# Fused attention and two-layer product on one Trainium2 core: the tenth pair of heads turned by DMA instead of on the matmul engine, with four edits around it

## The chip, the cores and the metric

The kernel runs on one core of a Trainium2 chip. A core has five engines with instruction queues of their own, which meet only at semaphores: PE (TensorE, matrix products), DVE (VectorE), ACT (ScalarE), POOL (GpSimd) and SP (SyncE, which here only issues DMA transfers). Sixteen DMA engines move the data; SP and ACT feed one group of queues, POOL another. The metric is the device time of one execution in microseconds, lower is better.

## The reference

The input is q, k and v, each of 8 batches x 12 heads x 448 rows x 64, a number tau of 0.1, w_in (768 x 2048) and w_out (2048 x 768), all float32.

```python
q_n = q / (norm(q, axis=-1) + 1e-6)
k_n = k / (norm(k, axis=-1) + 1e-6)
scores = q_n @ k_n.T / tau
attn = softmax(scores)                 # over the keys of one head
x = (attn @ v), heads side by side     # 3584 rows x 768
h = x @ w_in
out = maximum(0.01 * h, h) @ w_out     # 3584 x 768, float32
```

## The kernel before

**Pairs and quads.** Heads are worked two at a time. A pair s holds q and k of two heads; a batch has six pairs (NPAIR), so the pairs of batch 0 are 0 to 5, those of batch 1 are 6 to 11, and so on: the "tenth pair" is s = 9, the "ninth" s = 8. Two pairs form a quad j of four heads (pairs 8 and 9 are quad 4). The 448 rows are three tiles of 128 and a remainder of 64 rows.

**What a pair goes through.** `load_qk` (four transfers on SP's queue) or `load_pairs` brings the rows to `raw_sb`, which has six places, one for each pair of a batch. `squares` squares them, on POOL by default. `sums` adds them up on DVE, `roots` takes the roots on ACT, and `normalise` on DVE multiplies the rows with the reciprocals into `qn`, in bf16. `transposes` turns `qn` so that the 64 columns lie on the partitions: for s below DMA_FROM by seven PE transposes into one PSUM bank and a copy from there into `qkT`, from DMA_FROM on by one DMA transpose that SP issues. `norm` is roots, normalise, transposes and squares of a later pair in a row; its `hold` makes POOL wait for the rows of `qn`, so that what POOL does next starts behind them.

**Scores and exponents.** `key_tiles` makes the scores of one key tile of a pair on PE (two banks of PSUM) and their exponents on ACT. Tile 3 is the remainder tile: it takes the 64 remaining keys of both pairs of a quad at once, and its exponents go to `pr[j]`. `attend` and `attend_two` multiply the exponents with v and with ones; `attend_two` does two quads and begins with the remainder products of both, alternating between them (L306, `rem_products`).

**The first product** (`firsts`, L383): for each of 16 column blocks m of w_in six matmuls, and ACT's leaky ReLU (`Prelu`) into `hT`. The dictionary `between` says which steps of later pairs are written ahead of which m. The order in which the program is written is the order on every engine's queue.

**The second product** (`visit` with `groups`, L458) works through hT x w_out for one batch of tokens. While it runs, the key tiles of the next batch are put between its matmuls: `wide`, for the first visit, says after which step n a tile is put; pair 6's tiles come first, then pair 7's and so on to pair 11's. The visit begins with remainder tiles of some quads and ends with the others, behind the output copies of its last group, the first of which runs on ACT. The first group of the first visit goes through w_out in four parts of four row blocks, steps 1 to 16, 17 to 32, 33 to 48 and 49 to 64.

**w_out** comes in four quarters (`load_w_out`), issued on POOL's queue: quarters 0 and 4 behind the quad 2 results, quarters 8 and 12 in `norm` of pairs 7 and 8. The numbers are those of each quarter's first row block. On each kind of queue a transfer also waits for the landing of the eighth before it, since there are eight semaphores to tell of landings.

**The stretch of the change** is from 35 us, where batch 0's attention has ended, to 72 us, where batch 1's begins: firsts(0) with the norms of pairs 6 to 10, then visit(0).

The diff touches:

Of the kernel before, what the change touches and what calls it, by code (L numbers as in the profile page):

```python
# [16 lines left out]
def kernel(  # L17
# [10 lines left out]
    nc = tc.nc  # L28
# [11 lines left out]
    KT = D_model // 128  # L40
    MT = D_ff // 128
    HALF = D_model // 2
    DMA_FROM = 10
    WARM = 20
    SOON = 4
    AHEAD = 3
# [28 lines left out]
    def banks(count, keep=None, which=None):  # L75
        lo, hi = (0, 8) if not deals["apart"] else (0, 4) if count == 2 else (4, 8)
        x = which if which is not None else min(
            (i for i in range(lo, hi, count) if not set(range(i, i + count)) & set(sum(kept.values(), []))),
            key=lambda i: max(age[i : i + count]),
        )  # L80
        deals["n"] += 1
        age[x : x + count] = [deals["n"]] * count
        if keep:
            kept[keep] = list(range(x, x + count))
        return ps[:, x] if count == 1 else ps[:, x : x + count]
# [23 lines left out]
    def load_w_out(parts):  # L109
        for m in parts:  # L110
            gp.dma_start(out=w_out_sb[:, m : m + MT // 4], in_=w_out_r[:, m : m + MT // 4])

    def main(x, b, h0, nh):
        return x[b, h0 : h0 + nh, 0:MAIN].rearrange("h (p t) d -> p h t d", t=3)
# [22 lines left out]
    def load_qk(s):  # L137
        if s >= NSLOT:
            return
        b, h0 = s // NPAIR, 2 * (s % NPAIR)  # L140
        both = raw_sb[:, s % NPAIR]
        nc.sync.dma_start(out=both[:, :, 0:3], in_=main(q, b, h0, 2))
        nc.sync.dma_start(out=both[:, :, 4:7], in_=main(k, b, h0, 2))
        for i, x in enumerate((q, k)):
            nc.sync.dma_start(
                out=both[64 * i : 64 * i + 64, :, 3],
                in_=x[b, h0 : h0 + 2, MAIN:S].rearrange("h p d -> p h d"),
            )
        raw[s] = (both[:, :, 0:4], both[:, :, 4:7])
# [5 lines left out]
    def load_v(j):  # L155
        if j >= B * NQ:
            return
        b, jj = divmod(j, NQ)
        vb[j] = vbp.tile([128, 4, 3, D], BF16, name="v_b")
        gp.dma_start(out=vb[j], in_=main(v, b, 4 * jj, 4))  # L160

    def load_v_rem(b, parts=slice(0, 4)):
        if b >= B:
            return
        x = vrb[b % 2].rearrange("p j g d -> p (j g) d")
        for lo, h0, h1 in ((0, 0, 2), (64, 2, 6), (0, 6, 10), (64, 10, 12))[parts]:
            gp.dma_start(  # L167
                out=x[lo : lo + 64, h0:h1], in_=v[b, h0:h1, MAIN:S].rearrange("h p d -> p h d")
            )
# [3 lines left out]
    def squares(s, engs=(gp, gp)):  # L173
        if s >= NSLOT:
            return
        tiles = []
        for x, eng, name in zip(raw[s], engs, ("sq0", "sq1")):
            sq = sqp.tile(list(x.shape), F32, name=name)
            if eng is nc.scalar:
                nc.scalar.activation(sq, x, func=AF.Square)  # L180
            else:
                eng.tensor_tensor(sq, x, x, op=ALU.mult)  # L182
            tiles.append(sq)
        sqs[s] = tiles

    def sums(s, parts=(0, 1)):
        if s >= NSLOT:
            return
        if s not in ss:
            ss[s] = smp.tile([128, 14], F32, name="ss")  # L190
        for i in parts:
            o = ss[s][:, 0:8] if i == 0 else ss[s][:, 8:14]
            nc.vector.tensor_reduce(  # L193
                o.rearrange("p (h t) -> p h t", h=2), sqs[s][i], axis=AX.X, op=ALU.add
            )

    def roots(s):
        if s >= NSLOT:
            return
        nc.scalar.activation(ss[s], ss[s], func=AF.Ln, bias=tiny)  # L200
        nc.scalar.activation(ss[s], ss[s], func=AF.Exp, scale=0.5)  # L201

    qn, scalings = {}, {}
# [30 lines left out]
    def one(tp, s, lo, hi):  # L234
        for t in range(lo, hi):
            nc.tensor.matmul(
                out=tp[:, t, :],
                lhsT=qn[s][:, t].rearrange("p h d -> p (h d)"),
                rhs=id128,
                is_transpose=True,  # L240
                start=(t == lo),
                stop=(t == hi - 1),
            )

    def transposed():
        return banks(1).bitcast(BF16)[:, : 7 * 128].rearrange("p (t c) -> p t c", c=128)

    def transposes(s):
        if s >= NSLOT:
            return  # L250
        dst = qtp.tile([128, 7, 128], BF16, name="qkT")
        qkT[s] = dst.rearrange("p t c -> p (t c)")
        if s >= DMA_FROM:
            nc.sync.dma_start(
                out=dst, in_=qn[s].rearrange("p t h d -> p (t h d)"), transpose=True
            )
            return
        tp = transposed()
        one(tp, s, 0, 7)
        nc.vector.tensor_copy(out=dst, in_=tp)  # L260

    pe, pr = {}, {}

# [3 lines left out]
    def key_tiles(which):  # L267

        tiles = []
        for s, ki in which:  # L270
            sc = banks(2)
            tiles.append(sc)
            for i in range(2 if ki == 3 else 1):
                x = qkT[s - 1 + (i ^ s // 2 % NQ % 2)] if ki == 3 else qkT[s]
                for a in range(2):
                    rows = slice(64 * a, 64 * a + 64)
                    out = sc[64 * i : 64 * i + 64] if ki == 3 else sc
                    c0, c1 = (448, 512) if ki == 3 else (512 + 128 * ki, 640 + 128 * ki)
                    nc.tensor.matmul(  # L279
                        out=out[:, a, :S], lhsT=x[rows, c0:c1], rhs=x[rows, 0:S],  # L280
                        start=True, stop=True,
                    )
        for (s, ki), sc in zip(which, tiles):
            if ki == 3:
                pr[s // 2] = prp.tile([128, 2, S], BF16, name="pr")
                dst = pr[s // 2]
            else:
                if s not in pe:
                    pe[s] = pep.tile([128, 3, 2, S], BF16, name="pe")
                dst = pe[s][:, ki]  # L290
            nc.scalar.activation(out=dst, in_=sc[:, :, :S], func=AF.Exp, scale=inv_tau)  # L291
# [219 lines left out]
    def hold(x):  # L511
        seen = smp.tile([128, 1], F32, name="seen")
        gp.tensor_copy(out=seen, in_=x)  # L513
# [28 lines left out]
    dst = qtp.tile([128, 7, 128], BF16, name="qkT")  # L542
    qkT[0] = dst.rearrange("p t c -> p (t c)")
    for lo, hi in ((0, 4), (4, 7)):
        tp = transposed()
# [153 lines left out]
    def norm(s, transposed=True):  # L699
        if s >= NSLOT:  # L700
            return
        roots(s)
        normalise(s)
        if transposed:
            transposes(s)
        if s == 10:
            return
        for x in (12, 13) if s == 11 else (s + 4,) if s > 11 else ():
            load_qk(x)
        hold(qn[s][:, 6, 0, 0:1])  # L710
        if s < 9:
            load_w_out((4 * (s - 5),))
        if s == 11:
            squares(12)
        if s != 9:
            squares(s + (3 if s < 9 else 2))
# [11 lines left out]
    def visit(b, order, norms, between):  # L728


        s0 = (b + 1) * NPAIR
        tiles = [(s0 + p, ki) for p in range(NPAIR) for ki in range(3)]
        key_tiles([(s0 + 1, 3), (s0 + 3, 3)] + [(s0 + 5, 3)] * (b > 1))
        for i, (pairs, after) in enumerate(zip(order, between)):
            last = i == len(order) - 1
            for n, _ in enumerate(groups(b, pairs, 4 if len(pairs) > 1 else 1, last), 1):
                for _ in range(after.get(n, 0)):
                    key_tiles([tiles.pop(0)])
                for fn in norms.get((i, n), ()):
                    fn()  # L740
        assert not tiles
        if b < 2:
            key_tiles([(s0 + 5, 3)])

    def at(*steps):
        return {n: steps.count(n) for n in steps}
# [7 lines left out]
    attend(NQ - 1, [lambda m=m: first(0, m, range(KT - 2)) for m in range(3, SOON)])  # L754
    normalise(6)
    hold(xT[0][:, 2 * NQ - 2, 0:1])
    load_w_out((0, 4))
    hold(qn[6][:, 6, 0, 0:1])
    squares(9)
    norm(7, False)  # L760
    sums(8)
    firsts(
        0, SOON, {
            4: [lambda: transposes(6), lambda: norm(8, False)],
            6: [lambda: sums(9)],
            7: [lambda: transposes(7)],
            9: [lambda: norm(9, False)],
            10: [lambda: transposes(8)],
            11: [lambda: sums(10), lambda: load_v(3)],
            12: [lambda: norm(10), lambda: load_v(4)],  # L770
            13: [lambda: transposes(9), lambda: load_v(5), lambda: load_v_rem(1)],
            15: [lambda: sums(11)],
        },
    )
# [1 line left out]
    for b in range(B):  # L776
# [26 lines left out]
        s = ready  # L803
# [57 lines left out]
```

## Time and profile before

| | us |
|---|---|
| runs | 410.4, 408.26, 410.38; median 410.38 |
| profiled execution | 408.75 |
| its span | 407.0 |
| PE busy | 397.6 (98% of the span) |
| ACT busy | 262.3 (64%) |
| DVE busy | 191.1 (47%) |
| POOL busy | 143.5 (35%) |
| granted TensorE clock | 1.0 throughout |

A line of the timeline or of the lists has the start in us, the time it covers, the engine, the line of the kernel, the operation, what is written and read, the shape and the count; behind it in brackets stands the idle time of the engine before it and what ended that. In the waits, the numbers are total us, count and longest. PE's busy time is modelled for pipelined matmuls, so that 98% says that PE has hardly an idle moment, not that it works at its peak. A line of the chain of waits has start, length and what the chain went through.

### The profile page before, as it was taken

What the parts mean: (1) busy time and instruction counts of PE and PEld (TensorE: products, weight loads), DVE (VectorE), ACT (ScalarE), POOL (GpSimd) and SP (SyncE); (2) the same over time, 40 slices, a digit from 0 to 9 for tenths busy, and PEclk for the clock granted to TensorE, in tenths of its full rate; (3) what the DMA queues carried; (4) which work ended last, traced back from release to release, by engine and by line L of the source; (5) the groups of instructions that cost most, each with busy time, mean ns of one, the idle gap of its engine ahead of it and who ended that gap; (6) DMA issues with size and microseconds to landing.
All of it is one profiled execution on the core that took longest, in us unless ns stands there. A gap on an engine that the chain in (4) does not pass through costs nothing.

```text
span 407.0 us, 10163 instructions
## 1 busy us (share of the span) xinstructions
PE 397.6 (98%) x4086; PEld 225.0 (55%) x4096; DVE 191.1 (47%) x405; ACT 262.3 (64%) x454; POOL 143.5 (35%) x218
## 2 busy tenths in 40 slices
PE   7899999999999999999999999999999999999996
PEld 2335655444555655544786555544687555544554
DVE  5987931775674715355463626256262631130021
ACT  4995589566865579645876569845776559844300
POOL 4997632374325414253141622255122500000000
PEclk9999999999999999999999999999999999999999
DMA  7999999599598936588396854685397821110033
GB/s 181 248 224 240 216 180 229 154 177 203 124 199 160 156 72 159 118 131 176 58 183 154 125 128 109 168 117 134 81 168 129 102 46 40 40 41 2 0 78 79
DMA packets 100735, 54.21 MB, mean 133 GB/s; under 512 B 69424, under 2 KB 95440, under 8 KB 100688
## 3 DMA queue, kind: packets, MB, share of 16 engines
q1 hardware_dynamic: 76400, 40.13, 43.3%
q0 software_dynamic: 23440, 12.92, 23.3%
q8 instruction: 32, 0.52, 0.5%
q10 hardware_dynamic: 848, 0.52, 0.4%
q14 instruction: 15, 0.12, 0.1%
HBM read 45.61 MB, written 11.01 MB: 139 GB/s over the span
## 4 chain that ended last, share of the span: by engine, by line
PE 88%; DVE 5%; POOL 3%; DMA 1%; issue 1%; ACT 1%; POOLq 0%
PE ps L383 33%; PE ps L458 31%; PE ps L319 11%; PE ps L279 8%; PE ps L420 5%; DVE qn L222 2%; POOL sq L182 1%; PE ps L306 1%; DMA raw_sb<-in_k_dram 1%; DVE ss L193 1%; POOL v_rem L167 1%; DVE r L218 0%; DVE qkT L260 0%; POOL raw_sb L132 0%; DVE ss L217 0%
## 5 line engine op out<-in xcount | busy, mean ns | idle before, releaser
L383 PE MATMUL ps<-xT,w_in_sb 128*128 128x384 bf16 (+1 forms) x760 | 147.6, 352 | 0.4
L458 PE MATMUL ps<-w_out_sb,hT 64*128 64x384 bf16 x1536 | 144.0, 323 | 0.0
L291 ACT ACTIVATE pe<-ps 128x896 bf16<-128x896 f32 x144 | 124.5, 917 | 17.9 <-PE ps L279 16.0
L383 PEld LDWEIGHTS <-w_in_sb 128*128 128x128 bf16 x768 | 74.1, 98 | 71.7 <-issue 4.0
L390 ACT ACTIVATE hT<-ps 128x384 bf16<-128x384 f32 (+1 forms) x128 | 66.8, 543 | 66.4 <-PE ps L383 65.9
L458 PEld LDWEIGHTS <-hT 64*128 64x128 bf16 x1536 | 84.4, 94 | 44.6 <-PE ps L458 4.2
L182 POOL TENSOR_TENSOR sq<-raw_sb 128x512 f32<-128x512 f32 x92 | 84.9, 944 | 14.8 <-DMA raw_sb<-in_k_dram 13.9
L222 DVE TENSOR_TENSOR qn<-raw_sb,r 128x512 bf16<-128x512 f32 x96 | 59.2, 658 | 1.6
L279 PE MATMUL ps<-qkT 64*128 64x448 bf16 (+1 forms) x384 | 55.0, 353 | 2.1 <-DVE qkT L260 1.6
L193 DVE TENSOR_REDUCE ss<-sq 128x6 f32<-128x384 f32 (+1 forms) x95 | 54.3, 610 | 1.1 <-POOL sq L182 1.1
L470 DVE COPY osb<-ps 128x384 f32<-128x384 f32 x41 | 21.2, 553 | 69.8 <-PE ps L458 38.9
L513 POOL CAST seen<-qn 128x1 f32<-128x1 bf16 x47 | 9.2, 197 | 123.0 <-DVE qn L222 122.5
L217 DVE TENSOR_SCALAR ss<-ss 128x14 f32<-128x14 f32 x48 | 9.8, 205 | 74.0 <-ACT ss L201 73.8
L360 DVE TENSOR_TENSOR xT<-ps,rb 128x448 bf16<-128x448 f32 x48 | 27.8, 620 | 24.6 <-ACT rb L339 24.4
L160 POOL DMA_DIRECT2D v_b<-in_v_dram x24 | 18.6, 778 | 39.9 <-PE ps L319 39.9
L319 PE MATMUL ps<-pe,v_b 128*32 128x448 bf16 x576 | 32.0, 353 | 0.0
L279 PEld LDWEIGHTS <-qkT 64*128 64x128 bf16 (+1 forms) x384 | 17.8, 97 | 18.7 <-issue 7.3
L338 ACT ACTIVATE rb<-ps 128x448 f32<-128x448 f32 x24 | 12.9, 538 | 14.9 <-PE ps L319 13.9
L426 DVE COPY osb<-ps 128x384 f32<-128x384 f32 (+1 forms) x9 | 4.6, 513 | 36.6 <-issue 22.6
L319 PEld LDWEIGHTS <-v_b 128*32 128x32 bf16 x576 | 15.2, 97 | 11.9 <-issue 0.6
L291 ACT ACTIVATE pr<-ps 128x896 bf16<-128x896 f32 x24 | 20.8, 923 | 0.4 <-PE ps L279 0.4
L420 PE MATMUL ps<-w_out_sb,hT 128*128 128x384 bf16 (+1 forms) x144 | 21.0, 308 | 0.0
(50 smaller groups left out, 185.9 us busy)
## 6 DMA issues: line engine op xcount, KB each, us to landing
raw_sb<-in_q_dram SPq DMA_DIRECT2D x46, 192.0 KB, 3.3
raw_sb<-in_k_dram SPq DMA_DIRECT2D x44, 192.0 KB, 3.1
out_dram<-osb SPq DMA_DIRECT2D x30, 192.0 KB, 3.0
v_b<-in_v_dram POOLq DMA_DIRECT2D x24, 192.0 KB, 4.7
out_dram<-osb SPq DMA_DIRECT2D x12, 384.0 KB, 2.7
w_out_sb<-in_moe_w_out_dram POOLq DMA_DIRECT2D x4, 768.0 KB, 13.7
w_in_sb<-in_moe_w_in_dram POOLq DMA_DIRECT2D x3, 512.0 KB, 9.0
w_in_sb<-in_moe_w_in_dram POOLq DMA_DIRECT2D x2, 768.0 KB, 13.7
```

The lines of the kernel that those rows point to most:

```text
L182: eng.tensor_tensor(sq, x, x, op=ALU.mult)
L193: nc.vector.tensor_reduce(o.rearrange("p (h t) -> p h t", h=2), sqs[s][i], axis=AX.X, op=ALU.add)
L222: scalings[s] = nc.vector.tensor_tensor(qn[s][:, lo:hi], x.rearrange("p h t d -> p t h d"), r[:, r0 : r0 + 2 * nt].rearrange("p (h t) -> p ...
L279: nc.tensor.matmul(out=out[:, a, :S], lhsT=x[rows, c0:c1], rhs=x[rows, 0:S], start=True, stop=True,)
L291: nc.scalar.activation(out=dst, in_=sc[:, :, :S], func=AF.Exp, scale=inv_tau)
L319: nc.tensor.matmul(out=x[32 * g : 32 * g + 32, :S], lhsT=weights(g, ki) if ki < 3 else rem(g), rhs=pe[s][:, ki, a, :] if ki < 3 else pr[j] ...
L360: scalings[j, e] = nc.vector.tensor_tensor(xT[m][:, 2 * jj + e, half * S : (half + 1) * S], pos.pop((j, e))[:, :S], rbs[j], op=ALU.mult,)
L383: nc.tensor.matmul(out=pm[:, :n], lhsT=w_in_sb[:, kt, m * 128 : (m + 1) * 128], rhs=xT[c // 2][:, kt, c0 : c0 + n], start=(kt == 0), stop= ...
L390: nc.scalar.activation(out=hT[c][:, m, :n], in_=pms.pop((c, m))[:, :n], func=AF.Prelu, alpha=0.01)
L420: nc.tensor.matmul(out=po2[:, :n], lhsT=hT[c][:, m, ts * 128 : (ts + 1) * 128], rhs=w_out_sb[:, m, lo : lo + n], start=(m == 0), stop=(m = ...
L458: done[p][i] = nc.tensor.matmul(out=pos2[p][:, i, :HALF], lhsT=hT[c][rows, m, ts * 128 : (ts + 1) * 128], rhs=w_out_sb[rows, m, half * HAL ...
L470: copy(out=osb[c, ts][:, half * HALF : (half + 1) * HALF], in_=po2[:, i, :HALF])
```

## The change

DMA_FROM goes from 10 to 9, so pair 9 is turned by a DMA that SP issues, right behind its normalise, and its seven PE transposes and its copy on DVE are gone. The copy of pair 8 is done by ACT. Pair 9's squares are done by ACT, ahead of firsts(0), instead of by POOL. The remainder tile of pairs 8 and 9 goes from the beginning of the first visit to its end, ahead of that of pairs 10 and 11. The four quarters of w_out are issued one behind the other, without the hold on pair 6's rows that stood behind the first two. The transposes of pairs 6 and 7 are written one block of m later.

```diff
-    DMA_FROM = 10
+    DMA_FROM = 9
...
         tp = transposed()
         one(tp, s, 0, 7)
-        nc.vector.tensor_copy(out=dst, in_=tp)
+        copy = nc.scalar.copy if s > 7 else nc.vector.tensor_copy
+        copy(out=dst, in_=tp)
...
         hold(qn[s][:, 6, 0, 0:1])
-        if s < 9:
-            load_w_out((4 * (s - 5),))
...
-        key_tiles([(s0 + 1, 3), (s0 + 3, 3)] + [(s0 + 5, 3)] * (b > 1))
+        rests = [(s0 + i, 3) for i in (1, 3, 5)]
+        early = 1 if b == 0 else 2 if b == 1 else 3
+        key_tiles(rests[:early])
...
-        if b < 2:
-            key_tiles([(s0 + 5, 3)])
+        if rests[early:]:
+            key_tiles(rests[early:])
...
     hold(xT[0][:, 2 * NQ - 2, 0:1])
-    load_w_out((0, 4))
-    hold(qn[6][:, 6, 0, 0:1])
-    squares(9)
+    load_w_out(range(0, MT, MT // 4))
     norm(7, False)
+    squares(9, (nc.scalar, nc.scalar))
     sums(8)
     firsts(
         0, SOON, {
-            4: [lambda: transposes(6), lambda: norm(8, False)],
+            4: [lambda: norm(8, False)],
+            5: [lambda: transposes(6)],
             6: [lambda: sums(9)],
-            7: [lambda: transposes(7)],
-            9: [lambda: norm(9, False)],
+            8: [lambda: transposes(7)],
+            9: [lambda: norm(9)],
             10: [lambda: transposes(8)],
             11: [lambda: sums(10), lambda: load_v(3)],
             12: [lambda: norm(10), lambda: load_v(4)],
-            13: [lambda: transposes(9), lambda: load_v(5), lambda: load_v_rem(1)],
+            13: [lambda: load_v(5), lambda: load_v_rem(1)],
             15: [lambda: sums(11)],
         },
     )
```

## The prediction

> **What bounds the kernel now.** I read the page first, then the waits of the matmul engine, then its timeline and the chain of waits around the first visit, then the DMA view by stages.
>
> The page gives the matmul engine 397.6 us of 407.0, so all that an edit can win there is idle time or matmuls taken away:
>
> ```profile
> span 407.0 us, 10163 instructions
> ...
> PE 397.6 (98%) x4086; PEld 225.0 (55%) x4096; DVE 191.1 (47%) x405; ACT 262.3 (64%) x454; POOL 143.5 (35%) x218
> ```
>
> The waits of PE over the whole span have one item that the change touches, 0.8 us for a VectorE copy of a turned pair; the 1.2 us for qn are transposes that came early:
>
> ```profile
> PE ps L279 <- DVE qkT L260: 1.6, 3, 0.8
> ...
> PE ps L236 <- DVE qn L222: 1.2, 2, 1.1
> ```
>
> PE's timeline just ahead of the first visit shows the place: pair 9's seven transposes, the last 18 matmuls of the first product, the remainder tile of pairs 6 and 7, a hole, the remainder tile of pairs 8 and 9, and the visit's first matmuls on w_out.
>
> ```profile
> 47.30 0.79 PE L236 MATMUL ps<-id,qn 128*128 128x128 bf16 x7
> 47.94 3.09 PE L383 MATMUL ps<-xT,w_in_sb 128*128 128x384 bf16 x18
> 50.95 0.38 PE L279 MATMUL ps<-qkT 64*64 64x448 bf16 x4
> 52.14 0.38 PE L279 MATMUL ps<-qkT 64*64 64x448 bf16 x4 [0.81 <-DVE qkT L260]
> ```
>
> The chain says who makes the hole: VectorE, which works through norm, sums and copies of pairs 6 to 11 in order and puts pair 9's copy behind pair 10's norm.
>
> ```profile
> 50.39 1.16 DVE qn L222 x2
> 51.55 0.54 DVE qkT L260
> 52.10 0.04 issue
> 52.14 0.38 PE ps L279 x4
> ```
>
> From 52.46 to 71.9 PE has no hole, but its inputs come late. The w_out quarters, issued at 35.73, 36.53, 41.12 and 47.22 on POOL's queue, took 12.4, 15.4, 14.5 and 12.9 us to land; the view of their tile gives the ends. The view of qkT in the same stretch has the two turns by DMA, of pairs 10 and 11. The DMA view of 56 to 59 us shows that the two queues then send equal numbers of packets:
>
> ```profile
> DMA to landing us min/median/max: 12.4/13.7/15.4
> ```
>
> ```profile
> DMA to landing us min/median/max: 7.1/8.7/10.3
> ```
>
> ```profile
> q0 software_dynamic: 508, 0.34, 87.5%
> q1 hardware_dynamic: 516, 0.13, 51.7%
> ```
>
> So the quarters land at 48.15, 51.9, 55.65 and 60.1: 3.75 us apiece, and 4.5 us for the last, the one that runs beside pair 10's turn (issued 51.62, landed 61.9). PE's first matmul on each stands, counted off its timeline, at 52.46, 55.45, 58.62 and 61.78: spare 4.3, 3.5, 3.0 and 1.7 us.
>
> **The change part by part.** *Before the visit.* Pair 6's transposes go one block later: they start at 37.15 and the next block at 37.75, 18 matmuls take 2.93 us (40.68 less 37.75), so the twelve from 35.02 end at 36.97, and 0.78 us become the 0.39 that the unwaited transposes of pairs 7 and 8 show (43.99 to 44.38): 0.39 saved. Pair 9's transposes go: 0.63 (47.31 to 47.94). The hole and the second remainder tile leave this place: rest tile at 50.95, group from 51.14 (two tiles in a row follow at 0.19, as 68.12 and 68.31 do) instead of 52.46, but with the drain that one tile shows, 0.31, at 51.3: about 1.2. Sum 2.2: the visit starts at 50.25, if its feeders keep up.
>
> They do. ScalarE's squares of pair 9, 0.63 + 0.52 us from the start-up's rows, fall in its hole from 35.21 to 36.37 (1.16); if the cover fails, Prelus queue behind them, with eight banks to spare. VectorE loses two copies (0.61 each) and the norm of pair 7 that took 2.63 us beside POOL's squares at 37.85 to 40.12 becomes the usual 1.16. That brings pair 9's norm from 47.7 to about 46.7, pair 10's from 51.5 to about 50.0, pair 11's sums to 51.1. Pair 8's copy on ScalarE, 0.59 + 0.48 in the start-up's halves, stands behind the roots of pair 9 and ends near 45.9; PE first reads pair 8's rows at step n = 40 of the visit. PE waits for neither. The remainder of pairs 6 and 7 needs the copy of pair 7, at 44.6.
>
> *w_out's quarters in a row.* On POOL two issues of 0.8 us leave the path of the squares of pairs 10 and 11, but those wait for their rows until 44.86 anyway (a wait of 2.92 in the trace). Each issue waits for the landing of the one eight before it, here the two w_in halves (issued 25.65 and 26.45, landed 37.8 and 41.6), so POOL is free at 42.4. The queue has work without a break from 24 us, 3.75 us a quarter: an earlier issue lands nothing earlier. Zero; from below, if some of the 0.75 us by which the last quarter is stretched were late issue, it would win that.
>
> *Pair 9's turn.* Issued on SP near 46.7, on an empty queue; the next on SP is pair 10's turn, ready 3.4 us later. Unloaded a turn takes 2.9 us from issue to landing (78.59 to 81.55), loaded it took 10.3 and 7.1. First packets come 3.9 us after the issue when loaded (pair 10's: 55.55), so near 50.6. A turn is 128 x 896 bf16 in packets of some 256 bytes (0.13 MB in 516), so 896, 56 for each of 16 engines; a quarter of w_out has 128 x 4 rows, 32 an engine, one each 0.117 us (3.75 / 32). Alternating one for one, the quarter beside pair 10's turn took 0.75 us longer, 0.023 a packet of the turn. So quarter three, now also beside a turn, lands at 52.1 + 4.5 = 56.6 and quarter four at 61.1; pair 9's turn ends near 58.6, needed near 61. Bounds for the added delay at quarter four: 0, if the turns fit into gaps, and 1.65 us, a whole unloaded transfer (2.9 less the 1.25 of its issue); I take 0.95 (61.1 less 60.14), by the row nearest to it.
>
> The Trainium skill, "VectorE: DVE Perf Modes", section "The three transpose paths", speaks against the change: it gives 390 ns on TensorE and 1309 ns by DMA for a 128 x 128 tile, so that seven tiles would take an estimated 9.2 us a turn. The trace's unloaded 2.9 us for all seven contradicts it as a sum of tiles; with it for each of three turns in a row the last would end past 74 us and the sum be over +7.
>
> PE would reach quarter three at 56.4 and four at 59.6. It waits 0.2, then 1.4 us: at that place it is 0.6 us ahead of before, not 2.2.
>
> *The remainder tile at the end.* Before, only pair 11's stood there, read much later. Now that of pairs 8 and 9 stands there too, and the next matmuls on PE, the remainder products of L306, read its exponents at once (the second one does: they alternate between the two quads). ScalarE's rows there:
>
> ```profile
> 70.92 0.94 ACT L291 ACTIVATE pe<-ps 128x896 bf16<-128x896 f32 x1
> 71.72 0.51 ACT L470 COPY osb<-ps 128x384 f32<-128x384 f32 x1
> 72.08 0.97 ACT L291 ACTIVATE pr<-ps 128x896 bf16<-128x896 f32 x1
> ```
>
> The tile's scores start on PE at 71.57 and an exponent in that slot ends at 73.05, 1.48 us later; before, L306 started 0.31 later. With some 0.05 to be seen, PE loses 1.2 us there, and the added tile's own 0.19 hides in it. Bounds: 0.8, if the output copy were quicker out of the way, to 1.6, if the score tile's bank is late. Behind that wait PE's queue holds all products of the second batch; the other exponent, pair 11's, follows on ScalarE while PE works on the remainder products. From there to the end nothing changes, and PE has no hole there that could swallow the delay.
>
> *Pair 11's turn* is issued with the visit, 2.2 us earlier (57.05), behind those of pairs 9 and 10 on SP: pair 10's lands near 63.6 (needed 65.8), pair 11's near 67.2, where PE wants it at 67.5. Before: 66.35 against 68.12. I take no wait. The loads of pairs 12 and 13, next on SP, come no later than before, and the squares of pair 12 (68.39) with them.
>
> Sum: −2.2 + 0.2 + 1.4 + 1.2 = **+0.6 us**.
>
> The profiled execution took 408.75 us (span 407.0, 1.75 around it); the three runs, 410.4, 408.26 and 410.38, have a median 1.6 above it. So 409.35 against the profiled one, 411.0 against the median. As the runs lie on two levels, and the profile is of the lower, I say 410.8.
>
> **The rivals.**
>
> *The gain comes through.* The turn costs w_out nothing and the earlier issues keep quarter four at 59.6 or before; then −2.2 + 1.2 = −1.0: 407.75 by the profile, 409.4 by the median. For it: pair 10's turn is the only one seen beside w_out, so the 0.75 us may belong to the late issue of that quarter and not to the turn. Against: the fourth quarter's 4.5 us beside a turn. Even if ScalarE's exponent cost nothing, it ends at −2.2. Chance 0.2.
>
> *The turns queue one behind another, slower than before.* If three turns in a row each take the 6.3 us from first packet to landing of pair 10's (55.55 to 61.89), pair 9's ends at 57.0, pair 10's at 63.3 and pair 11's at 69.6, where PE wants it at 67.5: 2.1 us more, +2.7 in all, 411.45 by the profile, 413.1 by the median. It decides as soon as pair 11's turn lands after 67.5, 10.5 us after its issue; the 7.1 of before is against it, the 10.3 of pair 10's for it.
>
> *The hole was no hole.* The change may do nothing because VectorE still sets the pace (its norm of pair 10 at 51.5): then the start stays near 52.4, no wait for w_out arises, and +1.2 remains: 409.95 or 411.6. Against: nothing of pair 9 or 10 is read before 61 any more. Chance 0.05.
>
> **How the numbers follow.** The forecast has 0.47, the rivals 0.2, 0.28 and 0.05. What a measurement of this kernel can tell from no change is about 0.5%, 2 us. The forecast lies inside it, 0.85 of it with the spread of the runs (0.1 above, 0.05 below); the first rival has 0.6 inside and 0.4 faster, only because a low level may meet the high median; the second 0.7 slower; the third 0.8 inside. Sum: faster 0.10, same 0.65, slower 0.25. The range takes in the first rival by the median less half the spread of the runs and the second by the median: 408.4 to 413.1.
>
> **What would show it.** Right: no L260 copy and no 0.81 hole near 50 us; the visit's first w_out matmul near 50.3; a PE wait for w_out's last quarter of about 1 us near 60; a wait of L306 on ScalarE's exponent of about 1 us near 71; everything after shifted by a constant. Wrong if the last quarter lands before 60, if pair 11's tiles wait, or if L306 does not.

## The result: 0.3% faster, and the profile after

Over 22 runs of each, the changed kernel has a median of 408.73 us (407.71 to 409.84) and the kernel before one of 410.31 us (408.26 to 411.28). The ratio is 0.9968, with a 95% interval of 0.9956 to 0.9979: 1.3 us less. (It is the ratio of the means; the medians lie 1.6 us apart, since four of before's 22 runs were near 408.4.) That is inside the 0.5% named as no change and inside the range, but the forecast was +0.6 us, a time of 410.8, and the sign is the other one.

The runs of before did not spread evenly. Over this result and the experiments below there were 89 of them: 17 lie between 407.97 and 408.76, 72 between 409.85 and 411.55, and none between. The profiled execution of before (408.75) is of the lower, rarer kind. The two levels turn out to decide the sign.

The page of the changed kernel, its first lines. The span stands where that of before's profiled execution stood (407.0), with PE 0.6 us busier:

```profile
span 407.1 us, 10160 instructions
...
PE 398.2 (98%) x4089; PEld 225.8 (55%) x4089; DVE 187.9 (46%) x403; ACT 263.8 (65%) x457; POOL 140.5 (35%) x215
```

The waits of its PE (total, count, longest). The 0.8 us for the turned pair's copy is gone; a wait for w_out and one for ScalarE's exponent have come:

```profile
PE ps L459 <- DMA w_out_sb<-in_moe_w_out_dram: 1.2, 1, 1.2
PE ps L307 <- ACT pr L292: 0.7, 1, 0.7
```

Its PE timeline at three places: the visit's start, w_out's last quarter, and the moved remainder tile (lines after the edit count one higher: L279 is L280, L306 is L307). The first matmul of the remainder products runs at 71.15, the second only at 72.17:

```profile
49.77 0.38 PE L280 MATMUL ps<-qkT 64*64 64x448 bf16 x4
50.08 1.47 PE L459 MATMUL ps<-w_out_sb,hT 64*128 64x384 bf16 x16
...
58.96 0.67 PE L459 MATMUL ps<-w_out_sb,hT 64*128 64x384 bf16 x6
60.85 0.50 PE L459 MATMUL ps<-w_out_sb,hT 64*128 64x384 bf16 x4 [1.22 <-DMA w_out_sb<-in_moe_w_out_dram]
...
70.64 0.57 PE L280 MATMUL ps<-qkT 64*64 64x448 bf16 x8
71.15 0.36 PE L307 MATMUL ps<-pr,ones 64*32 64x448 bf16 x1
72.17 0.38 PE L307 MATMUL ps<-pr,ones 64*32 64x448 bf16 x7 [0.67 <-ACT pr L292]
```

The chain of waits now goes through the last quarter of w_out (issued 41.87, 18.93 us under way) instead of VectorE, and at the visit's end through the output copy and the exponent, as the prediction's slot said:

```profile
41.87 18.93 DMA w_out_sb<-in_moe_w_out_dram
60.80 0.04 issue
...
70.93 0.37 ACT osb L471
71.30 0.83 ACT pr L292
```

The tiles' landings, first w_out's quarters (47.89, 51.70, 56.24, 60.80; before 12.4 to 15.4 us), then the three turns (pair 9's at 59.86, pair 10's at 64.51, pair 11's at 67.27; before 7.1 to 10.3):

```profile
DMA to landing us min/median/max: 12.6/16.9/18.9
```

```profile
DMA to landing us min/median/max: 10.3/12.5/13.9
```

And the two DMA queues from 52 to 55 us, where before only w_out was under way; now pair 9's turn sends packet for packet with it:

```profile
q0 software_dynamic: 348, 0.51, 93.8%
q1 hardware_dynamic: 348, 0.09, 22.1%
```

Measured from the first matmul of `firsts(0)` (34.60 here, 35.02 in before's profile), the visit's first w_out matmul comes 1.96 us earlier, w_out takes 1.22 back, 0.23 goes in the visit, and the remainder tile takes 1.22: L307 resumes 0.71 us later than L306 did. (The whole times, 408.88 and 408.75, differ by 0.13 only, as `firsts(0)` began 0.42 earlier.) Against the execution it was worked out on, the forecast of +0.6 came true. What it was worked out on was not the usual execution.

### The profile page after: what moved, and what is told of

The parts are those of the page before. It is cut to its first block, busy times and chain, and to the rows that moved or that the text cites. A ratio compares the mean times of both kernels' runs of the same rounds, so it can differ in the third digit from the quotient of the medians.

```text
span 407.1 us, 10160 instructions
## 1 busy us (share of the span) xinstructions
PE 398.2 (98%) x4089; PEld 225.8 (55%) x4089; DVE 187.9 (46%) x403; ACT 263.8 (65%) x457; POOL 140.5 (35%) x215
## 4 chain that ended last, share of the span: by engine, by line
PE 82%; DMA 10%; POOL 3%; ACT 2%; issue 1%; DVE 0%; SPq 0%; POOLq 0%
PE ps L384 32%; PE ps L459 28%; PE ps L320 10%; PE ps L280 6%; PE ps L421 5%; DMA w_out_sb<-in_moe_w_out_dram 5%; DMA w_in_sb<-in_moe_w_in_dram 3%; POOL sq L182 2%; ACT pe L292 1%; DMA raw_sb<-in_q_dram 1%; PE ps L307 1%; DMA raw_sb<-in_k_dram 1%; POOL raw_sb L132 0%; POOL v_rem L167 0%; DVE qn L222 0%
## 5 line engine op out<-in xcount | busy, mean ns | idle before, releaser
L459 PEld LDWEIGHTS <-hT 64*128 64x128 bf16 x1536 | 85.4, 94 | 44.9 <-PE ps L459 4.0
L182 POOL TENSOR_TENSOR sq<-raw_sb 128x512 f32<-128x512 f32 x90 | 82.5, 937 | 15.2 <-DMA raw_sb<-in_k_dram 14.4
L222 DVE TENSOR_TENSOR qn<-raw_sb,r 128x512 bf16<-128x512 f32 x96 | 57.5, 640 | 2.0 <-DMA raw_sb<-in_q_dram 0.3
L280 PE MATMUL ps<-qkT 64*128 64x448 bf16 (+1 forms) x384 | 55.0, 353 | 1.1 <-DVE qkT L261 0.6
L217 DVE TENSOR_SCALAR ss<-ss 128x14 f32<-128x14 f32 x48 | 9.5, 198 | 74.8 <-ACT ss L201 74.7
L280 PEld LDWEIGHTS <-qkT 64*128 64x128 bf16 (+1 forms) x384 | 17.9, 97 | 17.5 <-issue 7.0
```

Of the source, the lines that this page charges most:

```text
L222: scalings[s] = nc.vector.tensor_tensor(qn[s][:, lo:hi], x.rearrange("p h t d -> p t h d"), r[:, r0 : r0 + 2 * nt].rearrange("p (h t) -> p ...
L280: nc.tensor.matmul(out=out[:, a, :S], lhsT=x[rows, c0:c1], rhs=x[rows, 0:S], start=True, stop=True,)
L459: done[p][i] = nc.tensor.matmul(out=pos2[p][:, i, :HALF], lhsT=hT[c][rows, m, ts * 128 : (ts + 1) * 128], rhs=w_out_sb[rows, m, half * HAL ...
```

## The experiments

They ran in four groups, each with runs of the kernel before on the same chip, whose medians were 410.42, 410.50, 410.23 and 410.31 us. Two runs far off, of 1069 us (the profiled one of the squares on ScalarE) and of 1130 us (one of the first attempt to force the meeting), are left out; why they took so long was not found.

**Before, unchanged, profiled twice more.** The second kernel differs in a comment alone.

> The kernel before, unchanged, profiled once more, because its first profile (408.75 us) was of the lower of its two levels and most runs took about 410.3. Late-rows theory: where the time is near 410.3, the hole on PE ahead of the first visit is not 0.8 us but 2.5 to 3 us, because the rows of pairs 10 and 11 land later, their squares, sums and norm come later, and pair 9's copy stands behind that norm on VectorE. Rival theory (elsewhere): the 2 us lie at the start-up, in the granted clock or in a later stage, and the hole stays at 0.8 us.

> The same again (only a comment added), for a second look at the usual level. Late-rows theory: hole of 2.5 to 3 us if the time is near 410.3, 0.8 if it is near 408.5. Elsewhere theory: the hole is 0.8 us at either level.

The first took 410.31 us, the upper level, the second 408.45, the lower. The upper one has the same 0.80 us hole before the visit, and its rows do not come late: pair 10's landed earlier (43.57 against 44.63 in the lower profile). What it has more is at pair 9's transposes, which ran almost without a wait at the lower level. Its PE timeline:

```profile
48.22 0.40 PE L236 MATMUL ps<-id,qn 128*128 128x128 bf16 x4 [0.95 <-DVE qn L222]
49.32 0.34 PE L236 MATMUL ps<-id,qn 128*128 128x128 bf16 x3 [0.70 <-DVE qn L222]
```

They wait for `normalise` of pair 9, two multiplies on VectorE. Here are VectorE's and then POOL's lines at the upper level; POOL's squares there are those of pair 11:

```profile
45.97 3.30 DVE L222 TENSOR_TENSOR qn<-raw_sb,r 128x512 bf16<-128x512 f32 x2
```

```profile
45.70 0.81 POOL L111 DMA_DIRECT2D w_out_sb<-in_moe_w_out_dram  x1
46.53 2.31 POOL L182 TENSOR_TENSOR sq<-raw_sb 128x512 f32<-128x512 f32 x2
```

And the same at the lower level, from before's profile. There the rows of pair 10 came later, so POOL's squares of pair 11 came behind the norm and fell beside VectorE's sums instead:

```profile
46.24 1.46 DVE L222 TENSOR_TENSOR qn<-raw_sb,r 128x512 bf16<-128x512 f32 x2
...
48.16 1.13 DVE L193 TENSOR_REDUCE ss<-sq 128x8 f32<-128x512 f32 x2
```

```profile
48.05 1.83 POOL L182 TENSOR_TENSOR sq<-raw_sb 128x512 f32<-128x512 f32 x2
```

The norm takes 3.30 us beside POOL's squares of pair 11, 1.46 ahead of them, and for the longer one PE pays 1.65 us (0.95 + 0.70). So the late-rows theory falls, and a new one, the collision theory, stands: at the upper level pair 9's norm runs into POOL's squares; the changed kernel no longer turns pair 9 on PE, so nobody waits for that norm, and the upper level is gone. The rival: some other edit of the change brings the gain.

**The change in parts.** First the remainder tile alone, in the kernel before:

```diff
-        key_tiles([(s0 + 1, 3), (s0 + 3, 3)] + [(s0 + 5, 3)] * (b > 1))
+        rests = [(s0 + i, 3) for i in (1, 3, 5)]
+        early = 1 if b == 0 else 2 if b == 1 else 3
+        key_tiles(rests[:early])
...
-        if b < 2:
-            key_tiles([(s0 + 5, 3)])
+        if rests[early:]:
+            key_tiles(rests[early:])
```

> The kernel before with one edit alone: the remainder tile of pairs 8 and 9 at the end of the first visit. Pair 9 is still turned on PE. Late-rows theory: nothing at the visit's start reads pair 9 any more, so the whole hole goes (2.5 to 3 us in the usual run, and 0.3 of the tile), and the wait on its exponent at the end costs 1.2: 1.5 to 2 us faster than before in the timing, ratio near 0.996. Elsewhere theory: only 0.8 + 0.3 go and 1.2 come, no difference, ratio 1.000.

410.45 us against 410.42, ratio 0.9997 (0.9973 to 1.0020), and both levels are there still: five of twelve runs at 408.15 to 408.87, seven at 410.43 to 412.25. The profile, of the upper level, has the norm of pair 9 at 3.30 us again, and L306 waits 0.7 us for the exponent. What the hole gives, the end of the visit takes.

Then the changed kernel with pair 9 turned on PE again:

```diff
-    DMA_FROM = 9
+    DMA_FROM = 10
...
-            9: [lambda: norm(9)],
+            9: [lambda: norm(9, False)],
...
-            13: [lambda: load_v(5), lambda: load_v_rem(1)],
+            13: [lambda: transposes(9), lambda: load_v(5), lambda: load_v_rem(1)],
```

> The changed kernel with one part undone: pair 9 turned on PE again (copied by ScalarE), all else as changed. If the DMA turn delays w_out's last quarter, as the forecast says, that quarter lands near 60.1 instead of 60.8, PE's wait of 1.2 us shrinks to 0.1 to 0.3 and the seven transposes cost 0.4: 0.3 to 0.6 us faster than the changed kernel. If the DMA turn is what brings the gain, it is at the level of before, 1.3 us slower than the changed kernel.

408.04 us, ratio 0.9954 (0.9937 to 0.9971), twelve runs within 407.8 to 408.33. The upper level is gone with pair 9 on PE, too, so the edit that names the change is not needed for that; it costs some 0.7 us instead of bringing anything. (The two kernels were not run in one group and the intervals of their ratios overlap, but 20 of the changed kernel's 22 runs lie above all twelve.) With PE turning the pair, w_out's last quarter landed at 59.21 and PE did not wait for it. Of the 1.59 us by which that is earlier, 0.86 were there at the first quarter already (47.03 against 47.89); the rest, some 0.7 us, goes with the turn.

The squares alone, in the kernel before:

```diff
-    squares(9)
     norm(7, False)
+    squares(9, (nc.scalar, nc.scalar))
```

> The kernel before with one edit alone: ScalarE squares pair 9, behind the norm of pair 7. Collision theory (formed on the first four runs): the usual level of before, 2 us above the lower one, is the norm of pair 9 on VectorE running beside POOL's squares of pair 11 (3.3 us in place of 1.2 to 1.4), with PE waiting for its rows. With the squares of pair 9 gone from POOL, the norm of pair 7 takes 1.2 in place of 2.6 us, all of VectorE's later steps come 1.5 us earlier, and the norm of pair 9 ends near 46.5 to 47 whether it collides or not: no PE wait over 0.3 us for its rows, one level of times near 408.3, ratio about 0.995. Rival (the move of pair 9 off PE, or of its remainder tile, is what counts): two levels as before, ratio 1.000.

408.14 us against 410.5, ratio 0.9940 (0.9918 to 0.9962): this edit by itself gives more than the whole change. A profile of it was taken later, below.

The quarters of w_out two and two again, in the changed kernel:

```diff
-    load_w_out(range(0, MT, MT // 4))
+    load_w_out((0, 4))
...
         hold(qn[s][:, 6, 0, 0:1])
+        if s < 9:
+            load_w_out((4 * (s - 5),))
```

> The changed kernel with one part undone: w_out's quarters issued two and two, the later ones in the norms of pairs 7 and 8 as before. Theory of the full queue: each quarter lands when the queue has come to it, so the last one lands near 60.8 as in the changed kernel, PE waits 1.2 us for it, and the time is the changed kernel's, 408.7, within 0.3 us. Rival (the earlier issue brings the last quarter in earlier): it lands 0.5 us or more later, and the time is longer by that.

408.67 us, the changed kernel's time. The last quarter was issued at 46.17 instead of 41.87 and landed at 59.88, no later, and 12.84 us behind the first one, which was 12.91 us in the changed kernel. The queue is full; an issue 4 us earlier buys nothing. PE waited 0.33 us for it, not the 1.2 expected, and 0.56 us for pair 11's turn.

**The collision by itself.** Three edits of the kernel before move POOL's squares of pair 11 about. In the first, they are held until pair 9's norm is done, and nothing else is touched:

```diff
-        if s != 9:
-            squares(s + (3 if s < 9 else 2))
+        if s != 8:
+            squares(11 if s == 9 else s + (3 if s < 9 else 2))
```

> The kernel before with one edit alone: POOL squares pair 11 only behind the rows of pair 9's norm (its hold), not before. Collision theory: the norm of pair 9 is free, 1.2 to 1.5 us, PE's wait for its rows is gone, and all times lie at the lower level or below, 408.4, ratio about 0.995; the squares may then meet the norm of pair 10, which PE reads later. Rival (level not from this collision): times as before on two levels, ratio 1.000.

408.32 us against 410.5, ratio 0.9947 (0.9929 to 0.9965), seven runs within 408.08 to 408.40: the upper level is gone, with pair 9 still on PE and the 0.80 us hole still in place. Its VectorE and POOL lines:

```profile
45.99 1.16 DVE L222 TENSOR_TENSOR qn<-raw_sb,r 128x512 bf16<-128x512 f32 x2
```

```profile
47.44 1.82 POOL L182 TENSOR_TENSOR sq<-raw_sb 128x512 f32<-128x512 f32 x2
```

In the second, the squares get ahead of the w_out issue that stood before them, so that they start earlier:

```diff
-        if s < 9:
+        if s < 8:
             load_w_out((4 * (s - 5),))
         if s != 9:
             squares(s + (3 if s < 9 else 2))
+        if s == 8:
+            load_w_out((12,))
```

> The kernel before with one edit alone: the issue of w_out's last quarter, 0.8 us on POOL between the squares of pair 10 and those of pair 11, goes behind the squares of pair 11. Collision theory: the squares of pair 11 start 0.8 us earlier, so also in executions in which the rows land late they run beside the norm of pair 9: nearly all times at the upper level, 410.4, the lower level (5 of 23 runs of before) gone or rarer; the profile shows that norm at 2.6 us or more and PE waiting over 1 us for its rows. Rival (the level is set by something that does not lie on POOL): times as before, a fifth of them near 408.4.

409.42 us, ratio 0.9974 (0.9956 to 0.9991); ten of twelve runs between 409.13 and 409.64, a level of their own and not the 410.4 expected. Its profile was of one of the two others (407.5). There pair 9's rows had come late, so that pair 7's norm met no squares and VectorE was some 1.5 us ahead; pair 9's norm met POOL's squares of pair 10 instead, and was stretched although it had begun first:

```profile
44.21 2.00 DVE L222 TENSOR_TENSOR qn<-raw_sb,r 128x512 bf16<-128x512 f32 x2
```

```profile
44.39 2.51 POOL L182 TENSOR_TENSOR sq<-raw_sb 128x512 f32<-128x512 f32 x2 [3.21 <-DMA raw_sb<-in_k_dram]
```

It ended at 46.21, before PE came to its rows (46.85), and so cost nothing: a stretched norm costs only what PE waits for it. On the ten this profile says nothing; another was taken:

> Another look at the kernel whose last w_out issue stands behind the squares of pair 11, which had 10 of 12 times at 409.1 to 409.6 and whose profile fell on one of the other two. Collision theory: at 409.4 the squares of pair 11 start at 45.7 instead of 46.5, so they meet the norm of pair 9 for its first half only, which takes 2.3 to 2.9 us instead of 3.3; PE waits 0.7 to 1 us less for its rows than at the upper level of before. Rival: that norm is free and the time lies elsewhere.

409.77 us, and the meeting is there, in half: the norm takes 2.43 us, and PE waits 1.31 us for it (0.61 + 0.70), 0.34 less than at the upper level, where 0.7 to 1 less was expected. VectorE's and POOL's lines; the first is the addition of L217, ahead of the norm:

```profile
45.13 0.85 DVE L217 TENSOR_SCALAR ss<-ss 128x14 f32<-128x14 f32 x1
...
46.29 2.43 DVE L222 TENSOR_TENSOR qn<-raw_sb,r 128x512 bf16<-128x512 f32 x2
```

```profile
46.04 2.27 POOL L182 TENSOR_TENSOR sq<-raw_sb 128x512 f32<-128x512 f32 x2
```

In the third, the meeting was to be forced, by a hold on pair 9's reciprocals, right ahead of its norm:

```diff
             nc.vector.reciprocal(r, r)
+        if s == 9:
+            hold(r[:, 0:1])
+            squares(11)
...
-        if s != 9:
+        if s not in (8, 9):
```

> The kernel before with POOL's squares of pair 11 tied to the moment in which VectorE begins pair 9's norm (POOL waits for its reciprocal), so that the two always run side by side; the counterpart of the run that holds these squares behind the norm (408.32 us). Collision theory: the norm of pair 9 takes 2.6 us or more in every execution, PE waits over 1 us for its rows, and all times lie on the upper level, 410.0 to 410.6, the lower one gone. Rival (holding the squares helped for another reason, such as the order of POOL's queue): as the held run, 408.3.

It missed: 408.27 us, ratio 0.9958 (0.9937 to 0.9979). The w_out issue (46.67 to 47.48) stood between, and the squares began at 47.62, behind the norm (45.69 to 47.16). That makes it one more run with the squares behind the norm, at the held kernel's time. So the issue was put behind the squares, too (`load_w_out((12,))` after `squares(11)`):

> The kernel before with POOL's squares of pair 11 tied to the reciprocal of pair 9's norm, and the last w_out issue put behind them, since that issue stood between the two in the run that was to force the meeting and let the norm end first. Collision theory: the squares start within 0.6 us of the norm in every execution, the norm takes 2.3 to 2.7 us, PE waits 1 to 1.5 us for its rows, all times on one level 1.0 to 1.5 us above the held kernel of this call, 409.3 to 409.9. Rival (the levels come from elsewhere): the held kernel's time.

408.28 us against 410.31, ratio 0.9953 (0.9939 to 0.9966): it missed again, and tells more. VectorE's line and POOL's:

```profile
46.01 1.16 DVE L226 TENSOR_TENSOR qn<-raw_sb,r 128x512 bf16<-128x512 f32 x2
```

```profile
46.10 0.64 POOL L517 COPY seen<-r 128x1 f32<-128x1 f32 x1 [0.44 <-DVE r L218]
46.70 2.15 POOL L182 TENSOR_TENSOR sq<-raw_sb 128x512 f32<-128x512 f32 x2
```

Here VectorE came first. The two engines take turns by whole instructions: POOL's copy of one column, otherwise 0.17 us, sat 0.64 us through the first multiply (46.01 to 46.70), the second went ahead, and POOL's squares took 2.15 instead of 1.82. POOL paid, VectorE did not. Meeting is not enough. In the five profiles in which pair 9's norm took 2.00 us or more (up to 3.30), the squares began before its first multiply had ended; here they began as it ended (46.70). So the collision was taken away and moved about, but never forced onto the upper level.

The squares on ScalarE, the held squares and the changed kernel were run again to close the account:

> Another look at the kernel before with the squares of pair 9 on ScalarE, whose times were 408.1 and whose profiled execution was disturbed from its start. Collision theory: norm of pair 7 at 1.2 us, norm of pair 9 ended by 47.3 whether it collides or not, PE's wait for its rows at most 0.4 us, time 407.5 to 408.3.

407.44 us. The norm of pair 9 took 1.41 us and began 1.0 us earlier than in the upper profile (44.99 against 45.97), since pair 7's norm took 1.16 us and not 2.62; PE did not wait for it, and the hole shrank to 0.20. Pair 11's squares came behind it (46.75).

> The kernel before with the squares of pair 11 held behind pair 9's norm, on the chip of the forced one and the changed one. Collision theory: one level near 408.3. It is the kernel before without the collision, so the prediction's sum of +0.6 us should be the changed kernel's time less this one.

> The changed kernel (only a comment added), beside the held one. If the prediction's sum was right for executions without the collision, it is 0.3 to 0.8 us slower than the held kernel, near 408.7. Rival (the sum was wrong as such and the change gains 1.3 us by itself): it is faster than the held kernel.

On one chip: held 408.15 us (0.9950, 0.9938 to 0.9963), changed 408.61 (0.9964, 0.9951 to 0.9976), before 410.31, where all nine runs of before were of the upper level. The changed kernel is 0.46 us slower than before without its collision, by the medians of five runs each (407.86 to 408.55 and 408.38 to 409.73). Where PE came to pair 9's rows before the norm was done or just behind it, and so not in the 407.5 us execution, the length of the norm and the time of the profiled execution go together: 1.16 to 1.46 us in those of before at 408.45 and 408.75 and of the held squares at 408.20 and 408.55; 2.43 with the squares ahead of the issue, at 409.77; 3.30 in before's at 410.31 and the tile's at 411.17.

**The two costs taken out.** The changed kernel with pair 9 on PE, as above, and the remainder tile of pairs 8 and 9 back at the start of the visit:

```diff
-        early = 1 if b == 0 else 2 if b == 1 else 3
+        early = 2 if b < 2 else 3
```

> The changed kernel with two parts undone: pair 9 is turned on PE (as in the run before, 408.04 us), and its remainder tile stands at the first visit's start again. ScalarE's copy of pair 9 ends near 49.5, before PE gets there at 50.4, so no wait there; PE's wait of 0.7 us for the exponent at the visit's end goes, with the 0.2 to 0.4 us that PE idles beside it: 0.8 to 1.1 us faster than the run with the tile at the end, near 407.1, the fastest of all. If the last quarter of w_out (landing near 59.2) now makes PE wait, the gain is smaller by that.

407.04 us (406.97 to 407.40), ratio 0.9919 (0.9900 to 0.9939) against before's 410.5: the best version, 3.3 us below before and 1.7 below the changed kernel. Its PE timeline shows the eight matmuls of both remainder tiles in one piece with no hole, and the remainder products at the end without a wait:

```profile
50.60 0.57 PE L280 MATMUL ps<-qkT 64*64 64x448 bf16 x8
51.11 1.47 PE L459 MATMUL ps<-w_out_sb,hT 64*128 64x384 bf16 x16
...
70.53 0.38 PE L307 MATMUL ps<-pr,ones 64*32 64x448 bf16 x8
```

The hole that the moved tile avoids is closed without the move: with pair 9's squares on ScalarE alone it had shrunk to 0.20, and here ScalarE makes the copies of pairs 8 and 9 (0.90 us each), too, pair 9's from 49.27. Which of the other edits closes the rest was not tried apart.

## Why the prediction was right and wrong

**Where it failed: the base of the sum.** "So 409.35 against the profiled one, 411.0 against the median." The difference of +0.6 was worked out on an execution of the lower level and then added to a median that belongs to the upper one, as if the 1.6 us between them lay outside the stretch that the change rewrites. They lie inside it. The term that was mis-sized by this is "Sum 2.2: the visit starts at 50.25": from the first matmul of `firsts(0)` the visit's w_out starts after 17.44 us in before's profile, after 19.19 in the upper one, after 15.48 in the changed kernel. The gain there is 1.96 us in the first case and 3.71 in the second. With the 2.67 us that come back later (1.22, 0.23 and 1.22), that is +0.71 or −1.04, and the second is the measured −1.3 within 0.3 us (the −1.6 of the medians within 0.6). Two other profiles with this turn (the quarters apart, and the changed kernel run again) come to the next `firsts` 0.32 and 0.66 us sooner after that first matmul than this one, so its waits are at the upper end. What ends the upper level is shown for one edit of the change: with pair 9's squares on ScalarE, and nothing else, the norm began 1.0 us earlier and was done before PE came. That the turn by DMA would end it alone, since PE then no longer reads that norm there, is likely and was not run. The prediction had both clues, two levels of runs and a norm (pair 7's) "that took 2.63 us beside POOL's squares", and did not ask which other norm could meet squares in the executions it had not seen. That 408.73 still lies in the range is luck: the lower end was there for a rival with another mechanism.

**"Before the visit" otherwise.** The start at 50.08 against 50.25 said is 0.24 us short of the sum, since `firsts(0)` began 0.42 earlier. Some 0.18 of that were never there to save: the 0.39 taken for pair 6's transposes counted them from 36.97, but here 18 matmuls from the start of `firsts(0)` take 3.11 us, not 2.93.

In the changed kernel the collision goes on, and moves; the norm of pair 9, from its profile:

```profile
44.67 2.60 DVE L222 TENSOR_TENSOR qn<-raw_sb,r 128x512 bf16<-128x512 f32 x2
```

That its cover holds was right: pair 9's rows are read only after 61, and no matmul waits for that norm.

**"w_out's quarters in a row": zero.** Right, by the run with the quarters apart.

**"Pair 9's turn": 0.2 + 1.4.** The queues alternate one for one as assumed. Quarter three landed at 56.24 (56.6 said) without a wait of PE, and four at 60.80 (61.1), and PE waited 1.22 (by its own figures, 61.1 less 59.8, the forecast should have had 1.3 there). The turns themselves were slower than said for pairs 9 and 10 (59.86 and 64.51 against 58.6 and 63.6) and as said for pair 11 (67.27 against 67.2). The wait is not the same in every execution: in two other profiles with this turn quarter four landed at 59.6 and 59.9, PE waited nothing and 0.33 us for it, and 0.6 us for pair 11's turn, for which no wait was forecast.

**"The remainder tile at the end": 1.2.** Right: scores at 70.64, L307 on at 72.17, 1.53 us later where before it was 0.31.

**The rivals.** "The gain comes through" gave 409.4 by the median, but by a quarter four at 59.6 that cost nothing; its time is near, its mechanism is not the one at work, since the tile's wait and a wait for a transfer are in every profile of the changed kernel. "The turns queue" would need pair 11's turn after 67.5 at a price of 2 us; of its mechanism 0.6 us is seen in two profiles. "The hole was no hole" falls with the start at 50.08.

**The figures for transposes.** The Trainium skill, "VectorE: DVE Perf Modes", "The three transpose paths", gives TensorE the shorter time for a 128 x 128 tile, 390 ns against 1309 by DMA. The kernel with pair 9 on PE is indeed some 0.7 us faster, but not by such times: seven transposes hold PE for 0.39 us (43.43 to 43.82), and what the profiles show of the turn by DMA is waits of PE for w_out's last quarter and for pair 11's turn.

## What to carry to other kernels

When the runs lie on two levels, find out which level the profile is of and profile the other one, before a sum is made: the difference between two executions of one kernel is a free experiment, and here it was 1.6 us, where 0.6 was forecast. A change of five edits can owe its gain to one that nobody counted (the squares moved to ScalarE) and lose part of it in the one it is named for; trying the edits one by one found a version with more than twice the gain. And an edit that moves work off an engine can also end its wait for a collision that only some executions show.

## What the runs showed of the hardware

VectorE's multiply with two inputs from SBUF and POOL's squares did not run side by side. The two multiplies of a norm take 1.16 us alone and up to 3.30 beside the squares. In the 407.5 us execution above, one by one: the first multiply has its usual 0.69 us (from 44.21), the first square begins beside it and takes 1.41 instead of 1.03 (from 44.39), the second multiply 1.39 instead of 0.55 (from 44.82), the second square 1.13 instead of 0.82 (from 45.77). That fits turns by whole instructions, in which the time of an instruction holds its wait for its turn. The sums, with one input, take 1.13 us beside the squares (48.16 in before's lines above) and 1.13 or 1.14 without.

One input alone does not keep an instruction out of it, though: the addition of L217, in place on 14 columns, took 0.85 us instead of 0.17 in the line shown above, and ended at 45.98, just behind the square beside it (45.13 to 45.95). In eleven more profiles it was stretched ahead of this norm (0.26 to 0.93 us), and each time it ended 0.03 to 0.04 us behind a square.

The Trainium skill, "GPSIMD Engine Reference", "1. Specifications", says that GpSimd's SBUF interfaces are shared with VectorE, with contention for VectorE instructions that have two SBUF inputs or run in a 2-port mode. For two inputs the traces agree, with the numbers above; whether L217's addition runs in such a mode no run here shows.

Two things stay open. The rows of pair 10 landed 8.74 and 8.93 us behind the first matmul of `firsts(0)` in the two profiles of the upper level (before's and the moved tile's) and 9.33 and 9.61 in the two of the lower, so they seem to choose the level; what makes them come sooner or later was not found. Nor why the first multiply of the upper profile, which started 0.56 us before POOL's first square, while POOL was issuing a transfer, ran for 2.20 us, when in the held kernel's two profiles it took 0.69 us beside such an issue; so who gets the first turn is not known in every case.
